# Fixed places for the fourth stage's split down weights, earlier decodings in the second stage, and two seams filled differently

## The chip, the core and the metric

The kernel runs on one core of one Trainium2 chip. A core has a matrix engine (TensorE, called PE in the rows), a vector engine (VectorE, DVE), a scalar engine (ScalarE, ACT), GpSimd (POOL) and a queue engine that issues transfers (SyncE, SP). Each engine works through its own list of instructions in order and waits on semaphores for the others. The metric is the device time of one execution in microseconds; less is better.

## The reference, cut to what matters

Three computations follow one another: a block-wise linear attention with decay, a mixture of four experts with ReLU, and a feed-forward block with SiLU.

```python
x = attention(q, k, v, lam)                 # 1536 tokens x 512
for e in range(4):                          # _moe_ref
    h = np.maximum(x @ w1[e], 0.0)          # 512 -> 1024
    out += p[:, e:e + 1] * (h @ w2[e])      # 1024 -> 512
h = out @ w_in                              # _moe2_ref, 512 -> 2048
g = h * (1.0 / (1.0 + np.exp(-h)))
return g @ w_out                            # 2048 -> 512
```

## The kernel before

All matmuls run in the fp32r format with each float32 operand split in two: a rounded high half and the rest as a low half. A product is then three matmuls (high by high, low by high, high by low). A **split** (`split`, line 145) is two instructions: ScalarE copies the source into the high half (line 149), and GpSimd, or VectorE, subtracts it from the source to give the low half (line 150). Every split therefore takes a place in ScalarE's list and one in GpSimd's.

The 1536 tokens are worked in four stages, which follow one another. Stage "a" does the mixture for the first 512 tokens, stage "c" the mixture for the other 1024, stage "b" the feed-forward for the first 512, stage "d" the feed-forward for the other 1024. In the order of time they are the first (a), second (c), third (b) and fourth (d). Stages c and d use a scheme with seven products instead of eight for a 2 by 2 block product.

Stage c has 16 steps. Its first eight run `pair_step` (line 823), the other eight `pair7` (line 1007), and stage d has eight steps of `pair7`. A step has seven **gaps**, 0 to 6. In each gap TensorE does one product of six matmuls (into a bank called x, z, y, y, z, x, y in turn), the step's own copies and vector work on that bank follow ("then" and "later" in the code), extra jobs given by the caller for that gap run (`prepare`), and then usually one **filler**: `filler` (line 744) takes the next down-projection piece from the list `fill` and lets TensorE do it. The third argument of `pair7` gives the number of fillers per gap. In gap 0 ScalarE copies x to y (line 1052), in gap 1 it copies z to s5 and in gap 2 y to s16 (line 1018); TensorE may go on with y in gap 2 only after the copy of gap 0, and with y in gap 3 only after the copy of gap 2. The four banks are handed on from step to step, so a step's x can begin when the former step's z has been read for the last time. At the end of a step the gated results are split as operands by `operand` (line 936): ScalarE makes the high half (line 940), VectorE or GpSimd the low half (line 942).

`unit` (line 736) is a clock that every product and every filler moves on by one; `after(n, fn)` lists `fn` to be issued n units later. The order of instructions on every engine is therefore written out by hand by the place of each call.

For `pair7` the down weights are first combined by `down_sums` (line 905, four GpSimd operations a step) and then split by `down_left(q)` (line 921; two copies on ScalarE and two subtractions on GpSimd for each q). Two steps make a group with seven such pieces, q = 7g to 7g+6. Each piece goes into one of six buffers used in turn, and the group's products (`down7`, line 966) are the fillers of the next two steps. `seven` (line 883) sets when pieces, sums and loads are issued: it ties them to units after the group's fillers, so that a piece can come ahead of the copy of gap 0 or of a sigmoid.

In the first eight steps of stage c the kernel also decodes weights of the last block from 64 bit words. `decode_next` (line 254) stores the result of the decoding before, loads words ahead and has ScalarE scale the upper words; `flush` (line 230) then issues the four VectorE instructions of the decoding (lines 207, 210, 213, 217). Fourteen decodings fall into stage c. Before the change they start in gap 4 of step 0, gaps 1 and 4 of steps 1 to 6, and gap 1 of step 7, and are flushed in gaps 0 and 3.

Between stages c and b (line 1338 on) the accumulated result is split into xhi and xlo, four columns each, and is then the moving operand of stage b's first product (`gemm1`, line 553). Six fillers stand between, three more follow stage b's first product and three its second; there a fourth call finds the list empty.

Of the kernel before, what the change touches and what calls it, by code (L numbers as in the profile page):

```python
# [31 lines left out]
NV = NF  # L32
# [7 lines left out]
def kernel(  # L40
# [97 lines left out]
    def load(j, n=1):  # L138
        for _ in range(n):
            if nxt[j] < len(seq[j]):  # L140
                ph, i, src = seq[j][nxt[j]]
                nxt[j] += 1
                (load_up, load_down)[j](src, i, (ph, i))
# [110 lines left out]
    def decode_next(more):  # L254

        if jobs[0] < 4 * NV:
            store_decoded()
            if more:
                load_next()
            pending.append(decode(jobs[0]))  # L260
            jobs[0] += 1
# [460 lines left out]
    def left_in2(i):  # L722
        t = leftp.tile([P, 2, 2, HW], F32R, tag="uc", name="uc")
        for n in range(2):
            nc.sync.dma_start(out=t[:, n].bitcast(F32), in_=wu[i][:, n, :2])
        grp_t[("d", i), 1] = t[:, 0], t[:, 1]
# [6 lines left out]
    def after(n, fn):  # L733
        due.append((clock[0] + n, fn))
# [9 lines left out]
    def filler():  # L744
        if fill:
            fill.pop(0)()
        unit()
# [135 lines left out]
    def seven(ph, first, n):  # L883

        now.update(ph=ph, first=first, groups=n // 2, dw=0, pending=None)
        free["o"] = list(range(9 if ph == "c" else 10))
        for box in (d_sums, dw_t, op_t, acc7, jobs7):
            box.clear()
        for g in range(n // 2):
            q = 7 * g  # L890
            todo = [(0, 1, lambda q=q: down_left(q + 6))]
            more = g + 1 < n // 2
            if more or ph == "c":
                todo.append((0, 5, lambda: load(1, 2)))
            if more:
                todo += [
                    (2, 1, lambda i=2 * g + 2: down_sums(i)),
                    (3, 1, lambda i=2 * g + 3: down_sums(i)),
                ]
                for m, when, n_ in ((4, 2, 7), (5, 2, 8), (5, 2, 9), (6, 1, 10), (6, 3, 11), (6, 5, 12)):  # L900
                    todo.append((m, when, lambda q=q + n_: down_left(q)))
            for m, when, fn in todo:
                jobs7.setdefault(q + m, []).append((when, fn))

    def down_sums(i):

        w = raw_t[(now["ph"], now["first"] + i), 1].rearrange("p n (d c) -> p n d c", c=HW)
        t = tmp["d"].tile([P, 3, HW], F32, tag="ds", name="ds", bufs=2)
        for to, a, b, op in (
            (t[:, 0], w[:, 0, 1], w[:, 1, 1], ALU.add),  # L910
            (t[:, 1], t[:, 0], w[:, 0, 0], ALU.subtract),
            (t[:, 2], w[:, 1, 0], t[:, 1], ALU.subtract),
            (w[:, 0, 1], w[:, 0, 0], w[:, 0, 1], ALU.subtract),
        ):
            nc.gpsimd.tensor_tensor(out=to, in0=a, in1=b, op=op)
        d_sums[i] = {
            1: w[:, 0, 0], 2: w[:, 1, 0], 4: w[:, 1, 1],
            5: t[:, 0], 6: t[:, 1], 3: t[:, 2], 7: w[:, 0, 1],
        }

    def down_left(q):

        turn = now["dw"] % 6
        now["dw"] += 1
        if turn < 2:
            t = tmp["op"].tile([P, 2, DM], F32R, tag="dw", name="dw", bufs=2)
        else:
            tag = ("dh", "dl")[turn % 2]
            t = wp.tile([P, 2, DM], F32R, tag=tag, name=tag)
        t = t.rearrange("p s (k c) -> p s k c", c=HW)  # L930
        for s in range(2):
            src = d_sums[q // 7 * 2 + s][ROUND[q % 7]]
            split(nc.gpsimd, t[:, s, 0], t[:, s, 1], src)
        dw_t[q] = t
# [216 lines left out]
    with tc.manual_schedule():  # L1151
# [149 lines left out]
        for i in range(NW):  # L1301
            jc = jobs_for(("c", i), ("c", i + 1) if i + 1 < NW else None)
            if i % 4 == 3:
                for gap, t in ((5, 1), (6, 0)):
                    jc.setdefault(gap, []).append(lambda t=t: load_gate("c", i // 4 + 1, t))
            if i < SW:
                for gap, fn in ((0, flush), (1, 0), (3, flush), (4, 0)):
                    if not fn:
                        if (i, gap) in ((0, 1), (SW - 1, 4)):
                            continue  # L1310
                        fn = lambda: decode_next(True)
                    jc.setdefault(gap, []).append(fn)
                if i == SW - 1:
                    jc[4].append(store_decoded)
                pair_step("c", i, jc)
                continue
            if i == SW:
                flush()
                store_decoded()
                words.close()  # L1320
                tmp["op"] = pool(ops, "opsp")
                fill[:] = fill[4:8] + fill[:4] + fill[8:]
                jc[4].insert(0, second_form)
                jc[5] = jc.get(5, []) + [lambda: down_sums(0)]
                jc[6] = jc.get(6, []) + [lambda: down_sums(1)]
            elif i == SW + 1:
                for gap, qs in ((0, [0]), (1, [1]), (3, [2]), (4, [3]), (6, [4, 5])):
                    jc.setdefault(gap, []).extend(lambda q=q: down_left(q) for q in qs)
            if i == NW - 1:
                jc[4] = [lambda: split_up(("b", 0), False)]  # L1330
            pair7(i - SW, jc, {SW: [1] * 7, SW + 1: [0, 1, 1, 1, 1, 1, 2]}.get(i))
# [7 lines left out]
        for d in range(KD):  # L1339
            split(nc.gpsimd, y_a[0][:, d], y_a[1][:, d], acc_t["a"][:, d])  # L1340
            if d % 2:
                filler()
        filler()

        nb = len(steps["b"])
        sums = ExitStack()
# [3 lines left out]
        for i in range(nb):  # L1350
            flush()
            gemm1("b", i)
            unit()
            if i < 2:
                for _ in range(3 + i):
                    filler()
            elif i < nb - 2:
                gemm2("b", i - 2)
            if i % 2:
                load(0)  # L1360
                left_out(i // 2)
                for n in ([0, 1] if i == 1 else [i // 2 + 1]):
                    if n < NV:
                        left_kept(n)
                if i == nb - 3:
                    grp_t[("d", 0), 0] = hi, lo = up_tiles(wp)
                    split(nc.gpsimd, hi[:, 0], lo[:, 0], lead[0])
                    split(nc.gpsimd, hi[:, 1:], lo[:, 1:], lead[1])
                if i < nb - 1:
                    split_down(("b", (i + 1) // 2))  # L1370
                else:
                    fill += last_down("b", nb)
                    filler()
            else:
                left_sums(("b", i // 2))
                if i == nb - 2:
                    left_in2(0)
                if 2 <= i < nb - 2:
                    split_up(("b", i // 2 + 1), False)
                if i == nb - 6:  # L1380
                    lead = [
                        leftp.tile([P, 2 * DM], F32, tag="uc", name="lead")[:, :HW],
                        tmp["sums"].tile([P, 4, HW], F32, tag="lead", name="lead"),
                    ]
                    nc.sync.dma_start(out=lead[0], in_=wd[0][0][:, A11 * HW:])
                    nc.sync.dma_start(out=lead[1], in_=wu[0][:, 2])
            if i == 1:
                assert not fill
                ops.close()
                tmp["sums"] = pool(sums, "sums2", side="right")  # L1390
            if i == 2:
                mixing = combine(acc_t["c", 0], acc_t["c", 1])
            elif i > 2:
                for job in mixing[i - 3:i - 2]:
                    job()
# [5 lines left out]
        for i in range(NV):  # L1401
            jobs = {}
            if i + 1 < NV:
                jobs[4] = [left_in(i + 1)]
                jobs[6] = [lambda: left_in2(i + 1)]
            if i == 0:
                jobs[0] = [lambda: down_sums(0)]
                jobs[2] = [lambda: down_sums(1)]
                jobs[5] = [lambda: down_left(0)]
            elif i == 1:  # L1410
                jobs[0] = [lambda: down_left(1)]
                jobs[4].insert(0, lambda: down_left(2))
                jobs[5] = [lambda: down_left(3), lambda: down_left(4)]
                jobs[6].append(lambda: down_left(5))
            pair7(i, jobs, {0: [0, 1, 1, 1, 0, 1, 0], 1: [0, 1, 1, 0, 1, 1, 2]}.get(i))
        fill[-1:] = [
            lambda o=o: down7(NV // 2 - 1, 6, 1, slice(o, o + CW))
            for o in range(0, TW, CW)
# [59 lines left out]
```

## Time and profile before

| | |
|---|---|
| median of three runs | 806.03 us (805.63 to 813.93) |
| the profiled execution | 806.18 us, of which 804.4 us from its first to its last instruction |
| mean granted clock of TensorE | 0.996 of full speed |
| TensorE busy | 785.6 us, 4038 matmuls |
| VectorE busy | 559.9 us, 803 instructions |
| GpSimd busy | 506.5 us, 458 instructions |
| ScalarE busy | 365.5 us, 656 instructions |

The profile page gives the busy time of each engine, its course over the span in 40 slices, the transfers, the chain of work that ended last, the costliest groups of instructions and the transfers by line. The trace behind it can be asked for the instructions in order of time, for the waits of an engine, and for the busy time and the granted clock in a stretch. "po<-ohi,dh" names the tile written and the tiles read; "x2" behind a row means that two equal neighbours were merged; square brackets give the idle time of the engine ahead of the row and what ended it. Times are microseconds from the first instruction.

### The profile page before, as it was taken

What the parts mean: (1) busy time and instruction counts of PE and PEld (TensorE: products, weight loads), DVE (VectorE), ACT (ScalarE), POOL (GpSimd) and SP (SyncE); (2) the same over time, 40 slices, a digit from 0 to 9 for tenths busy, and PEclk for the clock granted to TensorE, in tenths of its full rate; (3) what the DMA queues carried; (4) which work ended last, traced back from release to release, by engine and by line L of the source; (5) the groups of instructions that cost most, each with busy time, mean ns of one, the idle gap of its engine ahead of it and who ended that gap; (6) DMA issues with size and microseconds to landing.
All of it is one profiled execution on the core that took longest, in us unless ns stands there. A gap on an engine that the chain in (4) does not pass through costs nothing.

```text
span 804.4 us, 11063 instructions
## 1 busy us (share of the span) xinstructions
PE 785.6 (98%) x4038; PEld 645.7 (80%) x4038; DVE 559.9 (70%) x803; ACT 365.5 (45%) x656; POOL 506.5 (63%) x458
## 2 busy tenths in 40 slices
PE   9999999999999999998999999999999989999997
PEld 8888888788888888886888888878888767878786
DVE  7345587786685888887787878774555464677776
ACT  3323434324545333333444546463445576555551
POOL 3856646254774555555698988795877754565643
PEclk9999999999999999999999999999999999999999
DMA  7868768542344354332002121117676524232202
GB/s 295 311 221 251 233 212 299 197 156 92 102 161 137 112 158 131 130 103 93 15 27 105 42 90 57 49 52 269 222 260 225 181 87 138 77 100 83 81 1 106
DMA packets 39913, 113.89 MB, mean 142 GB/s; under 512 B 4482, under 2 KB 6706, under 8 KB 39858
## 3 DMA queue, kind: packets, MB, share of 16 engines
q1 hardware_dynamic: 39856, 113.18, 41.6%
q8 instruction: 32, 0.52, 0.3%
q14 instruction: 23, 0.19, 0.1%
q10 hardware_dynamic: 2, 0.00, 0.0%
HBM read 89.02 MB, written 24.14 MB: 141 GB/s over the span
## 4 chain that ended last, share of the span: by engine, by line
PE 73%; DVE 17%; ACT 6%; issue 2%; DMA 1%; POOL 1%; SPq 0%; ACTq 0%; POOLq 0%; DVEq 0%
PE ph L553 16%; PE po L609 16%; PE po L983 14%; PE y L755 8%; PE z L755 5%; PE x L755 5%; PE po L803 4%; DVE acc L817 3%; ACT hhi L782 2%; DVE olo L942 1%; DVE hlo L785 1%; PE s L419 1%; PE xps L458 1%; DVE dec L213 1%; DVE dec L207 1%
## 5 line engine op out<-in xcount | busy, mean ns | idle before, releaser
L150 POOL TENSOR_TENSOR ub<-u,ua 128x1024 fp32r<-128x1024 f32 (+2 forms) x41 | 70.2, 1712 | 107.4 <-ACT ua L149 94.7
L150 POOL TENSOR_TENSOR dl<-d,dh 128x1024 fp32r<-128x1024 f32 (+1 forms) x33 | 79.3, 2403 | 24.9 <-ACT dh L149 24.8
L150 POOL TENSOR_TENSOR ub<-us,ua 128x1024 fp32r<-128x1024 f32 x23 | 55.9, 2432 | 34.6 <-ACT ua L149 34.6
L579 ACT ACTIVATE hhi<-ph 128x512 fp32r<-128x512 f32 x40 | 23.9, 599 | 104.3 <-DVE ph L573 85.7
L947 DVE TENSOR_TENSOR acc<-po,acc 128x512 f32<-128x512 f32 (+1 forms) x77 | 51.8, 677 | 18.2 <-PE po L983 18.0
L609 PE MATMUL po<-hhi,dh 128*128 128x512 f32 (+1 forms) x208 | 57.2, 379 | 0.0
L609 PE MATMUL po<-hhi,dl 128*128 128x512 f32 (+1 forms) x208 | 55.9, 373 | 0.0
L609 PE MATMUL po<-hlo,dh 128*128 128x512 f32 (+1 forms) x208 | 55.9, 372 | 0.0
L553 PE MATMUL ph<-xhi,ua 128*128 128x512 f32 (+1 forms) x208 | 53.3, 378 | 0.7 <-DVE xlo L475 0.7
L553 PE MATMUL ph<-xlo,ua 128*128 128x512 f32 (+1 forms) x208 | 52.4, 373 | 0.4 <-POOL xlo L150 0.4
L553 PE MATMUL ph<-xhi,ub 128*128 128x512 f32 (+1 forms) x208 | 52.3, 373 | 0.0
L803 PE MATMUL po<-hhi,dl 128*128 128x512 f32 x128 | 50.0, 391 | 0.0
L803 PE MATMUL po<-hhi,dh 128*128 128x512 f32 x128 | 50.0, 391 | 0.0
L803 PE MATMUL po<-hlo,dh 128*128 128x512 f32 x128 | 49.9, 390 | 0.0
L580 DVE TENSOR_TENSOR hlo<-ph,hhi 128x512 fp32r<-128x512 f32 x40 | 27.7, 692 | 27.4 <-ACT hhi L579 27.4
L817 DVE TENSOR_TENSOR acc<-po,acc 128x512 f32<-128x512 f32 x56 | 36.9, 681 | 13.9 <-PE po L803 13.9
L149 ACT ACTIVATE dh<-d 128x1024 fp32r<-128x1024 f32 (+2 forms) x52 | 40.1, 791 | 8.7 <-PE po L609 3.6
L553 PEld LDWEIGHTS ph<-xlo,ua 128*128 128x128 f32 x208 | 37.4, 188 | 7.7 <-POOL xlo L150 0.9
L553 PEld LDWEIGHTS ph<-xhi,ua 128*128 128x128 f32 x208 | 36.8, 188 | 8.4 <-ACT xhi L474 0.9
L609 PEld LDWEIGHTS po<-hhi,dl 128*128 128x128 f32 x208 | 37.8, 188 | 7.1
L609 PEld LDWEIGHTS po<-hlo,dh 128*128 128x128 f32 x208 | 37.8, 188 | 7.0
L609 PEld LDWEIGHTS po<-hhi,dh 128*128 128x128 f32 x208 | 37.1, 188 | 7.5 <-issue 0.2
(219 smaller groups left out, 2160.0 us busy)
## 6 DMA issues: line engine op xcount, KB each, us to landing
u<-wts SPq DMA_DIRECT2D x32, 512.0 KB, 3.4
d<-wts SPq DMA_DIRECT2D x32, 512.0 KB, 4.5
words<-wts SPq DMA_DIRECT2D x32, 512.0 KB, 4.5
wd<-dec SPq DMA_DIRECT2D x32, 256.0 KB, 2.7
d<-wd SPq DMA_DIRECT2D x16, 512.0 KB, 3.8
qkt<-qk SPq DMA_DIRECT2D x12, 512.0 KB, 4.5
kvt<-kv SPq DMA_DIRECT2D x10, 512.0 KB, 4.6
u<-wd SPq DMA_DIRECT2D x8, 512.0 KB, 4.1
```

Of the source, the lines that this page charges most:

```text
L149: nc.scalar.activation(out=hi, in_=src, func=AF.Copy)
L150: eng.tensor_tensor(out=lo, in0=src, in1=hi.bitcast(F32), op=ALU.subtract)
L553: nc.tensor.matmul(pt[:, :n], lhsT=w, rhs=x[:, k, o:o + n], start=(j == 0), stop=(j == len(ops) - 1),)
L579: nc.scalar.activation(out=hi, in_=pt, func=AF.Copy)
L580: nc.vector.tensor_tensor(out=lo, in0=pt, in1=hi.bitcast(F32), op=ALU.subtract)
L609: nc.tensor.matmul(po_t[d][:, o:o + n], lhsT=w[:, d * P:(d + 1) * P], rhs=h[:, :n], start=(begin and j == 0), stop=(last and j == 2), skip ...
L755: nc.tensor.matmul(to, lhsT=a[:, k * P:(k + 1) * P], rhs=b[:, k], start=(first and j == 0), stop=(j == len(ops) - 1), skip_group_check=not ...
L782: nc.scalar.activation(out=hi, in_=c, func=AF.Copy)
L803: nc.tensor.matmul(po, lhsT=w, rhs=h, start=(j == 0), stop=(j == len(ops) - 1))
L817: nc.vector.tensor_tensor(out=a, in0=po, in1=a, op=ALU.add)
L947: eng.tensor_tensor(out=out, in0=a, in1=b, op=op)
L983: nc.tensor.matmul(po[:, part], lhsT=w, rhs=h[:, part], start=(fresh and j == 0), stop=(j == len(ops) - 1), skip_group_check=not fresh,)
```

## The change

It has three parts. In stage d, `seven` no longer lists anything; the caller gives every `down_left`, `down_sums` and `load` a gap of its own (`lefts` and `plan`), as a job behind that gap's copies. Pieces 0, 1, 2 and 3 of a group come in gaps 1, 2, 2 and 5 of the odd step ahead of the group, pieces 4, 5 and 6 in gaps 1, 1 and 2 of the even step that follows; the last two pieces come behind the last step. The fillers of step 0 move from gap 3 to gap 6. In stage c every decoding starts one place earlier: step 0 has one more, in gap 6, with a flush in its gap 5; step 6 has one more flush, in gap 6; step 7 has none. Between stages c and b one filler moves from behind stage b's second product to ahead of its first.

```diff
--- before.py
+++ after.py
@@ -886,12 +886,11 @@
         free["o"] = list(range(9 if ph == "c" else 10))
         for box in (d_sums, dw_t, op_t, acc7, jobs7):
             box.clear()
-        for g in range(n // 2):
+        for g in range(n // 2 if ph == "c" else 0):
             q = 7 * g
             todo = [(0, 1, lambda q=q: down_left(q + 6))]
             more = g + 1 < n // 2
-            if more or ph == "c":
-                todo.append((0, 5, lambda: load(1, 2)))
+            todo.append((0, 5, lambda: load(1, 2)))
             if more:
                 todo += [
                     (2, 1, lambda i=2 * g + 2: down_sums(i)),
@@ -1306,11 +1305,16 @@
             if i < SW:
                 for gap, fn in ((0, flush), (1, 0), (3, flush), (4, 0)):
                     if not fn:
-                        if (i, gap) in ((0, 1), (SW - 1, 4)):
+                        if (i, gap) == (0, 1) or i == SW - 1:
                             continue
                         fn = lambda: decode_next(True)
                     jc.setdefault(gap, []).append(fn)
-                if i == SW - 1:
+                if i == 0:
+                    jc[5].append(flush)
+                    jc.setdefault(6, []).append(lambda: decode_next(True))
+                elif i == SW - 2:
+                    jc.setdefault(6, []).append(flush)
+                elif i == SW - 1:
                     jc[4].append(store_decoded)
                 pair_step("c", i, jc)
                 continue
@@ -1340,7 +1344,8 @@
             split(nc.gpsimd, y_a[0][:, d], y_a[1][:, d], acc_t["a"][:, d])
             if d % 2:
                 filler()
-        filler()
+        for _ in range(2):
+            filler()
 
         nb = len(steps["b"])
         sums = ExitStack()
@@ -1352,7 +1357,7 @@
             gemm1("b", i)
             unit()
             if i < 2:
-                for _ in range(3 + i):
+                for _ in range(3):
                     filler()
             elif i < nb - 2:
                 gemm2("b", i - 2)
@@ -1403,16 +1408,24 @@
             if i + 1 < NV:
                 jobs[4] = [left_in(i + 1)]
                 jobs[6] = [lambda: left_in2(i + 1)]
+            lefts = {1: (1,), 2: (2,), 5: (3,)} if i == 1 else {1: (0,), 2: (1, 2), 5: (3,)}
+            if i % 2 == 0:
+                lefts = {1: (4, 5), 2: (6,)} if i else {}
+            elif i == NV - 1:
+                lefts[5] = (3, 4)
+            q = 7 * ((i - 1) // 2)
+            plan = [(gap, lambda n=n: down_left(q + n)) for gap, ns in lefts.items() for n in ns]
             if i == 0:
-                jobs[0] = [lambda: down_sums(0)]
-                jobs[2] = [lambda: down_sums(1)]
-                jobs[5] = [lambda: down_left(0)]
-            elif i == 1:
-                jobs[0] = [lambda: down_left(1)]
-                jobs[4].insert(0, lambda: down_left(2))
-                jobs[5] = [lambda: down_left(3), lambda: down_left(4)]
-                jobs[6].append(lambda: down_left(5))
-            pair7(i, jobs, {0: [0, 1, 1, 1, 0, 1, 0], 1: [0, 1, 1, 0, 1, 1, 2]}.get(i))
+                plan += [(0, lambda: down_sums(0)), (2, lambda: down_sums(1)), (5, lambda: down_left(0))]
+            elif i % 2 == 0:
+                plan += [(3, lambda: load(1, 2)), (5, lambda: down_sums(i))]
+            elif i > 1:
+                plan.append((0, lambda: down_sums(i)))
+            for gap, fn in plan:
+                jobs.setdefault(gap, []).append(fn)
+            pair7(i, jobs, {0: [0, 1, 1, 0, 0, 1, 1], 1: [0, 1, 1, 0, 1, 1, 2]}.get(i))
+        down_left(7 * NV // 2 - 2)
+        after(3, lambda: down_left(7 * NV // 2 - 1))
         fill[-1:] = [
             lambda o=o: down7(NV // 2 - 1, 6, 1, slice(o, o + CW))
             for o in range(0, TW, CW)
```

## Rows read from the trace of the kernel before

**Rows 1.** Page, first part: busy time (share of span) and instructions of each engine.

```profile
PE 785.6 (98%) x4038; PEld 645.7 (80%) x4038; DVE 559.9 (70%) x803; ACT 365.5 (45%) x656; POOL 506.5 (63%) x458
```

**Rows 2.** Waits of TensorE: who for whom, us in total, times, longest.

```profile
PE y L755 <- ACT y L1052: 4.6, 4, 3.0
...
PE po L983 <- DVE acc L947: 1.2, 2, 0.7
```

**Rows 3.** Timeline of TensorE, step 7 to 8 of stage c: start, us, instruction.

```profile
374.50 1.06 PE L755 MATMUL x<-hi,ua 128*128 128x512 f32 x2 [3.80 <-DVE hlo L785]
...
378.25 0.40 PE L803 MATMUL po<-hhi,dh 128*128 128x512 f32 x1
```

**Rows 4.** Timeline of VectorE, steps 2 and 7 of stage c.

```profile
251.43 0.42 DVE L207 TENSOR_SCALAR dec<-words 128x512 uint32<-128x512 uint32 x1
...
252.82 0.69 DVE L217 CUSTOM_DVE_ANT_0 dec<-dec,tail 128x1024 uint16<-128x1024 uint16 x1
...
364.57 2.14 DVE L207 TENSOR_SCALAR dec<-words 128x512 uint32<-128x512 uint32 x1
...
368.29 0.69 DVE L842 TENSOR_TENSOR v<-y,s 128x512 f32<-128x512 f32 x1
...
373.76 0.69 DVE L785 TENSOR_TENSOR hlo<-z,hhi 128x512 fp32r<-128x512 f32 x1 [0.74 <-ACT hhi L782]
```

**Rows 5.** Stretches: us, TensorE busy (matmuls), granted clock, transfer share, GB/s.

```profile
662.00:663.00 1.00, 0.20 (x1) 1.00 1.07 303
...
664.00:665.00 1.00, 0.00 (x0) 0.93 0.93 339
665.00:666.00 1.00, 0.81 (x2) 0.50 0.56 197
```

**Rows 6.** Timeline of all engines, steps 0 and 1 of stage c.

```profile
228.44 2.42 POOL L150 TENSOR_TENSOR ub<-us,ua 128x1024 fp32r<-128x1024 f32 x1 [0.21 <-ACT ua L149]
...
230.44 0.69 DVE L788 SCALAR_TENSOR_TENSOR x<-x,gate 128x512 f32<-128x512 f32 x1
...
230.83 2.40 POOL L150 TENSOR_TENSOR dl<-d,dh 128x1024 fp32r<-128x1024 f32 x1
...
233.13 0.60 ACT L782 ACTIVATE hhi<-y 128x512 fp32r<-128x512 f32 x1 [1.36 <-DVE y L788]
...
237.02 0.62 PE L755 MATMUL y<-hi,ua 128*128 128x512 f32 x2
```

**Rows 7.** Timeline of TensorE, stage b's first product.

```profile
539.84 0.50 PE L553 MATMUL ph<-xlo,ua 128*128 128x512 f32 x1 [0.45 <-POOL xlo L150]
```

**Rows 8.** Timeline of ScalarE and TensorE, steps 1 and 2 of stage d.

```profile
659.95 0.72 ACT L149 ACTIVATE dl<-d 128x256 fp32r<-128x256 f32 x2
660.56 0.60 ACT L628 ACTIVATE acc<-po 128x512 f32<-128x512 f32 x1
...
664.05 0.60 ACT L996 ACTIVATE acc<-po 128x512 f32<-128x512 f32 x1 [2.40 <-DMA out<-acc]
...
665.19 1.22 PE L755 MATMUL y<-hi,ua 128*128 128x512 f32 x2 [3.00 <-ACT y L1052]
```

**Rows 9.** Timeline of TensorE and ScalarE, steps 4 and 5 of stage d.

```profile
699.41 0.62 PE L983 MATMUL po<-hhi,dw 128*128 128x512 f32 x2
...
701.07 0.63 PE L755 MATMUL x<-hi,ua 128*128 128x512 f32 x2
...
707.70 1.32 ACT L149 ACTIVATE dw<-d 128x256 fp32r<-128x256 f32 x4
...
709.57 0.73 PE L755 MATMUL y<-hi,ua 128*128 128x512 f32 x2 [0.66 <-ACT s L1018]
...
721.94 0.61 PE L755 MATMUL x<-hi,ua 128*128 128x512 f32 x2
...
728.74 0.61 PE L755 MATMUL y<-hi,ua 128*128 128x512 f32 x2
```

**Rows 10.** Page, sixth part: transfers by line, KB each, us to landing.

```profile
d<-wd SPq DMA_DIRECT2D x16, 512.0 KB, 3.8
```


## What the change should do to the time

> **What bounds the kernel now.** First the page's busy times: TensorE is busy for 98% of the span [rows 1]. No other engine is near that, and the matmuls are the same after the change, so only TensorE's waits can be won or added, and what the clock loses behind them. Next TensorE's waits over the whole span: 4.6 us for the copy of gap 0 (line 1052), 3.0 of it at once, and 1.2 us for VectorE's additions [rows 2]. The timelines then show where the larger ones lie: 3.80 us between step 7 and 8 of stage c [rows 3], 0.45 us in stage b's first product [rows 7], 3.00 us in step 2 of stage d [rows 8], and small ones at each start of a group in stage d [rows 9]. One block of six matmuls is the unit: from x to the second y in step 5 of stage d are five blocks and no wait, 728.74 − 721.94 = 6.80 us, so 1.36 us a block and 0.227 us a matmul [rows 9].
>
> After the two long waits the clock matters too. Nine matmuls from 374.50 to 378.25 took 3.75 us where full speed gives 9 × 0.227 = 2.04 [rows 3]: 1.7 us more. In step 2 of stage d the granted clock is seen to fall to 0.50, 1.2 instead of 2.4 GHz. The last matmul had ended near 662.2 (busy 0.20 of the microsecond from 662), and the clock was still full until some 0.07 us ahead of 665 (0.93): it fell 2.7 us after the work had stopped [rows 5].
>
> **Stage c, step 7: −4.8.** Step 8's x waits for VectorE's low half of z at 373.76, the end of a chain that begins with v at 368.29, 5.47 us earlier [rows 4]. Ahead of v stood a decoding from 364.57, 3.72 us long, whose first instruction alone took 2.14 [rows 4]. Step 7 now has no decoding. v then waits for TensorE itself: the engine went idle at 374.50 − 3.80 = 370.70, and behind the product that v reads stood four blocks, so this ended near 370.70 − 4 × 1.36 = 365.26. v starts 368.29 − 365.2 = 3.1 us earlier, and x too; 0.7 us of wait are left, too short for a fall, so the 1.7 us come back: 3.1 + 1.7 = 4.8. Bounds: 3.1 (the clock falls anyway) and 5.5 (no wait left).
>
> **Stage c, step 0: +2.0.** The decoding taken from step 7 comes back at the other end. Step 0's flush stands ahead of the gating of x, which ran at 230.44 [rows 6], and nothing on VectorE covers it. Undisturbed a decoding takes 252.82 + 0.6 − 251.43 = 2.0 us [rows 4]. But GpSimd has two splits of 2.4 us in a row there, 228.44 and 230.83 [rows 6], and 2.14 us for an instruction that else takes 0.42 shows VectorE standing still behind such a split [rows 4]. I expect the first instruction when the first split ends (230.86), the second split from 231.2 to 233.5, and the other three (1.6 us) behind it: x is gated at 235.0, 4.6 late. Behind it on VectorE stand the low half of x and the gating of y; ScalarE's high half of y (233.13) moves to 237.7, and in ScalarE's list the copy of step 1's gap 0 is behind that: about 238.2 to 238.8. TensorE wants it at 237.02 [rows 6]: 1.8 us of wait and 0.2 to fill the engine again. Nothing wins this back, since TensorE is the bound. Bounds: an undisturbed decoding lets the copy end near 236.2, so 0; GpSimd's second split going first as well gives 2.2. I take 2.0, since the row with such a split beside it (2.14) is nearest.
>
> The Trainium skill speaks against this place (SBUF — State Buffer, "SBUF: two separate sides"): the port pair that VectorE and GpSimd share is a lock which an instruction holds to its end while the other one stands still. The 2.14 us agree; the page does not say who goes next, and if GpSimd did, the sum would be 797.5 instead of 797.3.
>
> Step 6's new flush runs about 355.4, ahead of the gating of y, in 2.0 us. The y copy of step 7 is 3 blocks ahead of its use, which hides it; without that cover it would cost up to 2.0. The other decodings keep their places with another job in them, nothing. In SP's queue one store and one load of words move ahead in step 0; behind them stand only loads for the next step, nothing.
>
> **Between c and b: −0.5.** One more block ahead of stage b's first product gives GpSimd 1.36 us more for xlo, and the wait was 0.45 [rows 7], with its restart 0.5. Behind the second product one block fewer stands; the operands there were split long before. Bounds 0 and −0.7.
>
> **Stage d, steps 0 to 2: −2.2.** The filler moved from gap 3 to gap 6 lets x and z of step 1 start earlier, but the second y then waits for the same copy to s16, ahead of which ScalarE has the same copies and one piece as before: nothing, bounds −0.6 and +0.3. In step 2 the 3.00 us go back to ScalarE, blocked at 664.05 for 2.40 us by the output transfer that frees the accumulator; this transfer starts behind the copy at 660.56 [rows 8]. That copy stood behind one piece (659.95, 0.61 us), which now comes later, and the pieces of gaps 4 and 5 ahead of it delayed it by about another 0.5 (one pair of copies, 0.6, less some slack; an estimate). So transfer, accumulator and y copy come 1.1 us earlier. TensorE's idle time shrinks to about 2.3 us, under the 2.7 after which the clock fell [rows 5]; I take it that the clock stays and about 1.5 us come back (seven matmuls at half speed, 7 × 0.227, the eighth in part). Pieces 4 and 5, four copies of together 1.3 us [rows 9], now stand ahead of s16: 0.4 lost. −1.1 − 1.5 + 0.4 = −2.2; bounds −0.7 (the clock falls) and −2.6.
>
> **Steps 3 to 7 and the end: −3.2.** Step 4 takes 709.57 − 701.07 = 8.50 us for the five blocks that take 6.80 in step 5, and its last filler ahead of x takes 701.07 − 699.41 = 1.66 instead of 1.36 [rows 9]: 2.0 lost, and step 6 has the same plan. The 0.3 and the wait for the copy of gap 0 come from pieces ahead of ScalarE's sigmoid of x and ahead of that copy; both move behind. The wait for s16 (0.66) stays, because four copies (1.32) still stand ahead of it [rows 9]. So 2.0 − 0.8 = 1.2 won in each, 2.4. In steps 5 and 7 one piece is new ahead of s16, 0.15 each: +0.3; in step 3 slack covers it. At the end the same earlier sigmoid wins 0.3 and the first of VectorE's late additions (0.7, restart 0.1 [rows 2]): −1.1. Buffers: a piece reuses the one six pieces before, whose last filler always runs at least one gap earlier, nothing. SP: the loads of down weights stay in gap 3, nothing; if they came late, see below. Together −3.2, bounds 0 and −3.8.
>
> **Sum.** −4.8 + 2.0 − 0.5 − 2.2 − 3.2 = −8.7. The profiled execution took 806.18 us (span 804.4, 1.8 around it): 797.5; the median of the runs is 0.15 lower, so 797.3.
>
> **Rivals.**
> - The decoding in step 0 costs nothing: VectorE is not stopped by the second split. For it, most decodings run beside GpSimd without TensorE waiting; against it, the 2.14 [rows 4]. 797.3 − 2.0 = 795.3. Chance 0.2.
> - The clock falls after the shorter idle times all the same, in stage d (+1.5), and perhaps in stage c (+1.7): 798.8 to 800.5. For it, 2.3 is not far below 2.7; against it, it has been seen only after more. Chance 0.18.
> - The fixed places only exchange waits: what leaves the copy of gap 0 goes to s16 and to the operands' high halves, behind which pieces now queue in gap 5. Steps 3 to 7 win nothing, 797.3 + 3.2 = 800.5. For it, ScalarE has the same copies in sum; against it, step 5, which had few pieces ahead of its copies and no wait. Chance 0.13.
> - Slower: the pieces' copies wait in ScalarE's list for the down weights and their sums, with all copies behind them, in steps 3, 5 and 7. The weights are asked for in gap 3 of the even step and read first in gap 1 of the odd one, ten blocks or 13.6 us later, and take 3.8 [rows 10]; GpSimd's sums lie between. To cost all 8.7, each step has to lose 2.9: it decides from weights and sums ready 12.7 us late instead of 3.8 after the issue plus 13.6 − 3.8 = 9.8 of slack, less the sums. Then 806 and more. Chance 0.04.
>
> **How the numbers follow.** The forecast has 0.45, its own range 796.2 to 798.6. The range goes from the free decoding to both falls or the exchanged waits, 794.8 to 800.5, and leaves out no more than 2 in 10. A measurement of this kernel tells about 1% (8.06 us) from no change; that is 797.97, close above the forecast. Faster by more: about 0.3 of the 0.45 and the 0.2, so 0.5; within 1%: 0.46; slower: 0.04.
>
> **What would show it.** Step 7: no line 207 from 358 on, step 8's x near 371 and a granted clock of 1.00 behind it. Step 0: line 207 at 230.5 standing behind a split, and a wait of TensorE for line 1052 near 237. Stage b: no wait for xlo. Stage d: line 996 still waiting for the transfer, about 1.1 us earlier, the clock at 1.00; no wait for line 1052 in steps 4 and 6, but one of about 0.7 for line 1018. The prediction is wrong if TensorE waits in step 0 or 1 of stage c for longer than 2.6 us, or in steps 3, 5 or 7 of stage d behind a piece.

## The result, and the profile after

The changed kernel took 798.11 us (median of 20 runs, 795.98 to 805.53) against 806.14 us for the kernel before in the same runs (805.43 to 813.93): a ratio of 0.989, 95% interval 0.986 to 0.992. The forecast was 797.3 (range 794.8 to 800.5). The profiled execution has a span of 796.4 us instead of 804.4. In the profiles of five experiments below a VectorE instruction stands for 7 to 8 us, in one of them twice (last section), and by their times some executions of every kernel here seem to hold such a standstill, so stretches are compared, not spans, and a time called undisturbed leaves those executions out.

The page's busy times of after, and the longest of TensorE's waits over its span (who for whom, us in total, times, longest; a line of before between 894 and 1308 has a number smaller by one in after):

```profile
PE 781.7 (98%) x4038; PEld 644.6 (81%) x4038; DVE 557.2 (70%) x803; ACT 365.0 (46%) x656; POOL 502.9 (63%) x458
```

```profile
PE y L755 <- ACT y L1051: 2.8, 2, 2.2
PE y L755 <- ACT s L1017: 1.8, 3, 0.7
PE y L755 <- ACT y L833: 1.6, 1, 1.6
...
PE x L755 <- DVE hlo L785: 0.9, 1, 0.9
...
PE po L982 <- DVE acc L946: 0.5, 1, 0.5
```

Against [rows 1, 2] TensorE's 4038 matmuls fill 781.7 us instead of 785.6. Of these 3.9 us, 1.6 are matmuls behind step 7 that ran at the slow clock before (below). The rest was not traced in full; a matmul's end is modelled, so part of a wait counts as busy (the wait listed as 0.45 in [rows 7] is 0.61 from start to start, as worked out below for the part between c and b). Of the four waits for the copy of gap 0, 4.6 us, two are left, 2.8 us; the 3.80 us between steps 7 and 8 of stage c [rows 3] have become 0.9; one wait of 1.6 us (line 833) is new.

TensorE does the same matmuls in both kernels, so the start of the same matmul in the two traces tells at each point how far after is ahead. The last column is what the part in between gave:

| up to, in TensorE's list | start before | start after | ahead | forecast of the part | measured |
|---|---|---|---|---|---|
| stage c, step 0, last filler ahead of the late y | 236.80 | 236.54 | −0.26 | – | −0.26 |
| first filler behind that y | 238.38 | 239.99 | +1.61 | +2.0 | +1.87 |
| step 8, z | 378.95 | 375.81 | −3.14 | −4.8 | −4.75 |
| stage b, a product at 589 | 589.18 | 585.25 | −3.93 | −0.5 | −0.79 |
| stage d, step 2, last filler ahead of the late y | 661.81 | 657.62 | −4.19 | ↓ | −0.26 |
| step 2, y of gap 3 | 669.47 | 664.60 | −4.87 | −2.2 (with the row above) | −0.68 |
| last accumulation but one | 800.21 | 792.25 | −7.96 | −3.2 | −3.09 |

The sum is −8.0 instead of −8.7, and one part carries the difference: stage d, steps 0 to 2, gave 0.94 instead of 2.2. The 0.26 of the first row lies ahead of everything that the change touches.

**Stage c, step 7.** Timelines of VectorE and TensorE of after:

```profile
366.73 0.70 DVE L842 TENSOR_TENSOR v<-y,s 128x512 f32<-128x512 f32 x1 [0.73 <-PE y L755]
...
372.19 0.69 DVE L785 TENSOR_TENSOR hlo<-z,hhi 128x512 fp32r<-128x512 f32 x1 [0.74 <-ACT hhi L782]
...
372.94 0.72 PE L755 MATMUL x<-hi,ua 128*128 128x512 f32 x2 [0.87 <-DVE hlo L785]
...
375.13 0.39 PE L803 MATMUL po<-hhi,dh 128*128 128x512 f32 x1
```

In step 7 no line 207 stands ahead of v any more; v now waits for TensorE itself (its releaser is "PE y"). The chain from v to z's low half still takes 372.19 − 366.73 = 5.46 us, as in [rows 4]. The wait is 0.87 instead of 3.80, and the nine matmuls behind it take 375.13 − 372.94 = 2.19 us; in before they took 3.75 [rows 3]. The clock stayed, with 1.00 granted in each of the three microseconds from 373. It is so in all ten traces: the three that keep the wait of 3.8 us (before, and below "stage d alone" and "the filler alone") have the fall behind it, the seven with 0.9 have none.

**Stage c, step 0.** GpSimd, VectorE, ScalarE and TensorE of after, in order of time:

```profile
228.18 2.42 POOL L150 TENSOR_TENSOR ub<-us,ua 128x1024 fp32r<-128x1024 f32 x1 [0.20 <-ACT ua L149]
230.19 0.69 DVE L207 TENSOR_SCALAR dec<-words 128x512 uint32<-128x512 uint32 x1
230.57 2.57 POOL L150 TENSOR_TENSOR dl<-d,dh 128x1024 fp32r<-128x1024 f32 x1
230.81 2.62 DVE L210 TENSOR_SCALAR tail<-words 128x512 uint32<-128x512 uint32 x1
233.34 0.68 DVE L213 SCALAR_TENSOR_TENSOR dec<-words,dec 128x512 uint32<-128x512 uint32 x1
...
234.67 0.69 DVE L788 SCALAR_TENSOR_TENSOR x<-x,gate 128x512 f32<-128x512 f32 x1
...
237.35 0.60 ACT L782 ACTIVATE hhi<-y 128x512 fp32r<-128x512 f32 x1 [0.82 <-DVE y L788]
237.85 0.59 ACT L833 ACTIVATE y<-x 128x512 f32<-128x512 f32 x1
...
238.49 0.73 PE L755 MATMUL y<-hi,ua 128*128 128x512 f32 x2 [1.56 <-ACT y L833]
```

The second of the decoding's four instructions stands for 2.62 us and ends 0.3 us after GpSimd's second split does (233.14). Everything behind it moves as the forecast said: x is gated at 234.67, against 230.44 in [rows 6], the y copy of line 833 starts at 237.85 and TensorE waits 1.56 us. The forecast had named line 1052 for this wait; that copy belongs to `pair7`, and `pair_step`, which runs here, has its own at line 833.

**Stage d, step 2.** ScalarE, SyncE and TensorE of after, and the stretches of a microsecond around the late y (us, TensorE busy, granted clock, transfer share, GB/s):

```profile
655.70 0.59 ACT L628 ACTIVATE acc<-po 128x512 f32<-128x512 f32 x1
656.32 0.34 SPq L629 DMA_DIRECT2D out<-acc  x1
...
659.03 0.60 ACT L995 ACTIVATE acc<-po 128x512 f32<-128x512 f32 x1 [1.87 <-DMA out<-acc]
659.53 0.59 ACT L1051 ACTIVATE y<-x 128x512 f32<-128x512 f32 x1
...
660.17 1.22 PE L755 MATMUL y<-hi,ua 128*128 128x512 f32 x2 [2.17 <-ACT y L1051]
```

```profile
658.00:659.00 1.00, 0.00 (x1) 1.00 1.02 215
659.00:660.00 1.00, 0.00 (x0) 1.00 0.88 312
660.00:661.00 1.00, 0.83 (x2) 0.59 0.67 242
661.00:662.00 1.00, 1.00 (x3) 0.50 0.09 32
```

The copy that starts the transfer runs at 655.70 instead of 660.56 [rows 8]; less the 3.8 us that TensorE is ahead at step 1, that is 1.1 us earlier, as forecast. The wait shrinks from 3.00 to 2.17. But the clock falls again, to 0.50, and the 1.5 us that were to come back with it did not.

### The profile page after: what moved, and what is told of

It reads as the page before. It is cut to its first block, busy times and chain, and to the rows that moved or that the text cites. A ratio compares the mean times of both kernels' runs of the same rounds, so it can differ in the third digit from the quotient of the medians.

```text
span 796.4 us, 11068 instructions
## 1 busy us (share of the span) xinstructions
PE 781.7 (98%) x4038; PEld 644.6 (81%) x4038; DVE 557.2 (70%) x803; ACT 365.0 (46%) x656; POOL 502.9 (63%) x458
## 4 chain that ended last, share of the span: by engine, by line
PE 85%; DVE 6%; ACT 4%; issue 2%; DMA 1%; POOL 1%; SPq 0%; ACTq 0%; DVEq 0%
PE po L982 17%; PE ph L553 15%; PE po L609 14%; PE po L803 11%; PE y L755 11%; PE z L755 6%; PE x L755 6%; PE s L419 2%; PE xps L458 1%; DVE olo L941 1%; ACT ohi L939 1%; PE xps L454 1%; DVE s L946 1%; DVE sg L946 1%; PE xps L487 0%
## 5 line engine op out<-in xcount | busy, mean ns | idle before, releaser
L553 PEld LDWEIGHTS ph<-xhi,ub 128*128 128x128 f32 x208 | 37.4, 188 | 7.0
```

The lines of the kernel that those rows point to most:

```text
L553: nc.tensor.matmul(pt[:, :n], lhsT=w, rhs=x[:, k, o:o + n], start=(j == 0), stop=(j == len(ops) - 1),)
```

## The experiments

After was not run beside the kernels below. The kernel before was, and took 807.12 us beside the first four and 806.79 beside the other four, against 806.14 beside after. So a difference of about 1 us between the medians of after and of an experiment shows nothing by itself; there the traces decide.

### Each part alone

**The decodings alone.** The kernel before with only the change in stage c:

```diff
-                        if (i, gap) in ((0, 1), (SW - 1, 4)):
+                        if (i, gap) == (0, 1) or i == SW - 1:
...
+                if i == 0:
+                    jc[5].append(flush)
+                    jc.setdefault(6, []).append(lambda: decode_next(True))
+                elif i == SW - 2:
+                    jc.setdefault(6, []).append(flush)
```

> The kernel before with the earlier decodings of stage c alone. Theory (the parts add up; step 7's wait of 3.8 us and the slow matmuls behind it are won, a wait of 1.6 us in step 1 is paid): 4.8 won, 1.8 lost, so 3.0 us less than the kernel before, near 803.1, and the profile shows TensorE waiting 1.6 us for line 833 near 237 and about 0.9 us for a low half of x at step 8, with the clock at full speed there. Rival (the decodings' gain comes from the stages behind, and stage c alone only moves the wait from step 8 to step 1): within 1 us of the kernel before, near 805.5.

Measured: 802.68 (12 runs, 801.01 to 811.2), before 807.12 beside it; ratio 0.996 (0.9925 to 0.9995). That is 4.4 us less where 3.0 were expected, but the interval, 0.4 to 6.0 us, holds both. TensorE of this kernel, at steps 0 and 8:

```profile
239.41 0.73 PE L755 MATMUL y<-hi,ua 128*128 128x512 f32 x2 [1.57 <-ACT y L833]
...
373.86 0.72 PE L755 MATMUL x<-hi,ua 128*128 128x512 f32 x2 [0.88 <-DVE hlo L785]
```

Both waits are those of after to a hundredth: gain and loss belong to the decodings, and neither needs the rest of the change. In its trace step 0 costs 1.9 us and step 7 gives 4.7, as in after.

**Stage d alone.** After, with the decodings and the filler between c and b as in before:

```diff
-                        if (i, gap) == (0, 1) or i == SW - 1:
+                        if (i, gap) in ((0, 1), (SW - 1, 4)):
...
-        for _ in range(2):
-            filler()
+        filler()
...
-                for _ in range(3):
+                for _ in range(3 + i):
```

> The kernel before with the fixed places of stage d alone. Theory (pieces behind the copies take away the waits for the copy of gap 0 at each group's start and the late sigmoid of x; the wait for the output transfer stays): 4.1 us less, near 802.0, of it 3.1 in steps 3 to 7 and the end, 1.0 in steps 0 to 2; if the clock stays up in step 2, 1.4 us less again. Rival (the waits are only exchanged, line 1052 against line 1018): within 1 us of the kernel before in steps 3 to 7, near 805.

Measured: 801.64 (7 runs, 799.76 to 815.29), ratio 0.993 (0.989 to 0.997). TensorE of this kernel, with step 2's late y, the next y, and the y of gap 3 in step 4; and two stretches behind the first:

```profile
678.23 0.72 PE L755 MATMUL y<-hi,ua 128*128 128x512 f32 x2 [2.02 <-ACT y L1051]
...
681.46 0.73 PE L755 MATMUL y<-hi,ua 128*128 128x512 f32 x2 [0.19 <-ACT s L1017]
...
720.34 0.73 PE L755 MATMUL y<-hi,ua 128*128 128x512 f32 x2 [0.51 <-ACT s L1017]
```

```profile
678.00:679.00 1.00, 0.77 (x3) 1.00 0.83 294
679.00:680.00 1.00, 1.00 (x6) 1.00 0.05 18
```

Steps 4 and 6 behave as in after (no wait for line 1051, one of half a microsecond for line 1017). Step 2 behaves as the forecast said and after's profile did not: the clock stays at 1.00, and behind it a small wait for s16 shows. From the product at 589 of the table above to the y of gap 3 in step 2 this kernel takes 77.75 us, before 80.29 and after 79.35: 2.5 won where the forecast had 2.2.

**The filler alone.** The kernel before with only this:

```diff
-        filler()
+        for _ in range(2):
+            filler()
...
-                for _ in range(3 + i):
+                for _ in range(3):
```

> The kernel before with the filler between stages c and b alone. Theory: TensorE's wait for xlo (0.45 us listed, 0.7 from start to start) goes and nothing else: 0.7 us less, near 805.4. Rival (stage b's third product, with one filler fewer ahead of it, waits for the split of its own weights instead): no change, 806.1.

Measured: 810.84 (12 runs, 805.01 to 818.28), ratio 1.001 (0.998 to 1.005). By time this is inconclusive: the interval is wider than the 0.7 us in question. The trace decides: it has no wait of stage b's product for GpSimd's low half any more, and none in its place, and the stretch from the last fillers of stage c (527.67 in before) to the product at 589 takes 60.75 us instead of 61.51, exactly as in after: 0.76 won.

### What costs 1.8 us in step 0

Two edits move one of the two things that met there: the decoding, or the second of GpSimd's two splits.

**The extra decoding in step 5** (after, changed so):

```diff
-                if i == 0:
-                    jc[5].append(flush)
-                    jc.setdefault(6, []).append(lambda: decode_next(True))
+                if i == SW - 3:
+                    jc.setdefault(6, []).extend([flush, lambda: decode_next(True)])
```

> The changed kernel, with the extra decoding in gap 6 of step 5 instead of step 0 (both its flush and its start), where GpSimd has no split. Theory (step 0's cost comes from VectorE's decoding standing behind two splits of GpSimd ahead of the gating of x): the 1.6 us wait for line 833 goes and none takes its place, 1.8 us less than the changed kernel, near 796.3. Rival (any third decoding ahead of a gating makes the next step's copy late by its 2 us, wherever it stands): a wait of 1 to 2 us appears at step 6's gap 2 instead and the time stays near 798.1.

Measured: 796.38 (6 runs, 794.57 to 803.24), ratio 0.987 (0.983 to 0.992). No wait for line 833 is left, and no new one of its size took its place. In its trace 1.86 us are won in step 0, and 0.35 are lost again at the first y of step 7 (360.19), where the copy of line 833 now comes just too late.

**The splits of step 0 earlier** (after, changed so; `split_down` is the second of the two splits, with its copy on ScalarE, and the first stays):

```diff
-            jobs[5 if key[1] < SW - 1 else 3] = [lambda: split_down(key)]
+            jobs[5 if 0 < key[1] < SW - 1 else 3] = [lambda: split_down(key)]
...
-                    jc[5].append(flush)
+                    jc.setdefault(5, []).append(flush)
```

> The kernel after, with the GpSimd splits of step 0 of the second stage in gap 3 instead of 5, so that the second of them does not stand beside VectorE's early decoding; the decoding and the flush stay in gap 5. Theory (GpSimd's splits on the same operands' memory hold VectorE's decoding up, each by its own length): the decoding takes about 2.3 us less, the wait for y at step 1 falls to 0.3 or less, 1.6 to 1.8 us less than after: near 796.4. Rival (the decoding's own 2 us ahead of the gating is what costs): a wait of more than 1 us stays, 798.1.

Measured: 798.73 (4 runs, of which the two undisturbed took 795.34 and 796.71), ratio 0.988 (0.983 to 0.993). By time this is too few runs; the trace decides. GpSimd, VectorE and TensorE of this kernel at the same place:

```profile
228.20 2.41 POOL L150 TENSOR_TENSOR ub<-us,ua 128x1024 fp32r<-128x1024 f32 x1 [0.21 <-ACT ua L149]
230.21 0.69 DVE L207 TENSOR_SCALAR dec<-words 128x512 uint32<-128x512 uint32 x1
230.82 0.41 DVE L210 TENSOR_SCALAR tail<-words 128x512 uint32<-128x512 uint32 x1
...
232.48 0.69 DVE L788 SCALAR_TENSOR_TENSOR x<-x,gate 128x512 f32<-128x512 f32 x1
...
236.79 0.62 PE L755 MATMUL y<-hi,ua 128*128 128x512 f32 x2
```

The decoding starts at the same time, in the same place of VectorE's list, and delays the gating of x by 2.3 us instead of 4.5: its second instruction takes 0.41 instead of 2.62, and TensorE waits for nothing. Not the decoding's own 2 us are the price, but the split of GpSimd that runs beside it. Not every VectorE instruction pays it: in before the gating of x (230.44) ran beside the same two splits in its usual 0.69 us [rows 6].

### What is left in stage d

**An accumulator of its own** (after, changed so; the place that stage d's first accumulator shares with stage b's output is what the transfer has to free):

```diff
-                acc_t["d"] = accp.tile([P, KD, TW], F32, tag="acc", name="acc")
+                acc_t["d"] = tmp["d"].tile([P, KD, TW], F32, tag="accd", name="acc")
```

> The kernel after, with the fourth stage's accumulator in a tile of its own instead of the place that the output still being transferred holds. Theory (the wait of TensorE for y at step 2, 2.2 us in after, goes back to the output transfer through the accumulation on VectorE, and the slow clock behind it costs the rest of the 4.0 us of slips there): the accumulation no longer waits for the transfer, the wait and the slow stretch go, a wait of 0.4 to 0.9 for the copy of s appears at steps 1 and 2, so about 3.3 us less than after: near 794.8. Rival (the copies of y are late by ScalarE's own work, or by the PSUM place, and the transfer is only the last of several): another wait of like size takes its place, and the time stays at 798.

Measured: 795.68 (8 runs, 794.57 to 803.35), ratio 0.984 (0.980 to 0.987). The transfer was named right as cause, with one word of the expectation wrong: the accumulation that waited is ScalarE's line 995, not VectorE's. ScalarE and TensorE of this kernel:

```profile
664.65 0.59 ACT L995 ACTIVATE acc<-po 128x512 f32<-128x512 f32 x1
665.13 0.61 ACT L1051 ACTIVATE y<-x 128x512 f32<-128x512 f32 x1
...
665.79 0.73 PE L755 MATMUL y<-hi,ua 128*128 128x512 f32 x2 [0.21 <-ACT y L1051]
...
669.48 0.73 PE L755 MATMUL y<-hi,ua 128*128 128x512 f32 x2 [0.67 <-ACT s L1017]
```

Line 995 waits for nothing, and TensorE 0.21 us instead of 2.17. Behind it the wait for s16 shows in full, 0.67. The gain is smaller than expected, though: the median is 2.4 under after's instead of 3.3. In the traces the 13 matmuls from the last filler ahead of that y to the y of gap 3 take 4.29 us instead of 6.98, 2.7 less, and where after's clock stays up there is less to win (table below).

**Piece 5 in gap 2** (after, changed so):

```diff
-                lefts = {1: (4, 5), 2: (6,)} if i else {}
+                lefts = {1: (4,), 2: (5, 6)} if i else {}
```

> The kernel after, with piece 5 of an even step's splits in gap 2, behind piece 6's place, so that one piece and not two stands in gap 1. Theory (the waits of 0.5 to 0.7 us for the copy of s at the even steps of the fourth stage come from the piece that stands ahead of it on VectorE): they shrink at steps 4 and 6, about 1.0 to 1.2 us less than after: near 797.0. Rival (the copy of s is late by its own chain from the hidden product, whatever stands ahead): no change, 798.1.

Measured: 797.10 (6 runs, 794.25 to 802.49), ratio 0.987 (0.983 to 0.991): 1.0 us under after's median, which by itself could be chance. The trace decides: the y of gap 3 in step 4, which waited 0.50 us at 703.35 in after, starts without a wait at 708.15 here, and so does that of step 6 (746.74). The waits came from the pieces ahead of the copy; the rival fell. The place is ScalarE's list, which the expectation called VectorE's: in after four copies of line 149 stand there from 701.49 to 702.72, here two.

**All three** (the extra decoding in step 5, the accumulator, piece 5):

> The kernel after with the extra decoding and the flush moved to step 5 of the second stage (as in the earlier run that did this alone), the fourth stage's accumulator in a tile of its own, and piece 5 of the even steps in gap 2. Theory (three separate stalls at three places): the gains add, 1.8 + 3.3 + 1.2 less than after, 791.5 to 792. Rival (they share a cause, or one stall takes another's place): 793.5 or more.

Measured: 791.80 (6 runs, 791.02 to 797.2), ratio 0.980 (0.976 to 0.984): faster than both kernels. The waits of TensorE in it:

```profile
PE x L755 <- DVE hlo L785: 0.9, 1, 0.9
PE y L755 <- ACT y L1051: 0.8, 2, 0.6
PE po L982 <- ACT hhi L939: 0.8, 1, 0.8
PE z L755 <- DVE sg L946: 0.7, 1, 0.7
PE y L755 <- ACT s L1017: 0.7, 1, 0.7
```

The longest wait in the stages c, b and d is 0.9 us. The median lies 6.3 us under after's, with 6.3 expected. Step by step in the traces: 1.5 us are won in stage c as by the extra decoding alone, 3.6 in stage d up to the y of gap 3 in step 2 (the accumulator alone: 2.9), and 1.0 behind it (piece 5 alone: 1.1). So the gains add, and 0.6 come on top: piece 5 in gap 2 also takes away most of the wait for s16 that the accumulator had laid bare (0.07 instead of 0.67). That the sum met the expectation to a tenth is luck, since the accumulator had been put too high.

## Why the prediction was right, and where it was not

**TensorE as the only bound: right.** Every gain and loss found is a wait of TensorE or its clock behind one.

**Step 7, −4.8: right (−4.75)**, by both of its terms: v released by TensorE, and the slow matmuls gone.

**Step 0, +2.0: right (+1.87)**, and so is the mechanism, which was the least certain, in its order too. The first instruction of the decoding, 0.42 us when undisturbed [rows 4], takes 0.69 and ends at 230.88, 0.28 us after the first split (230.60); the second split follows, and the second instruction ends at 233.43, 0.29 after it (233.14). The 2.14 us on which the forecast rested [rows 4] ended at 366.71, likewise 0.28 after this split of before:

```profile
364.03 2.40 POOL L150 TENSOR_TENSOR dl<-d,dh 128x1024 fp32r<-128x1024 f32 x1 [0.57 <-ACT dh L149]
```

x is gated at 234.67; less the 0.26 that after is ahead there, it is 4.5 late, forecast 4.6. The Trainium skill (SBUF — State Buffer, "SBUF: two separate sides") says that the shared port pair is held for a whole instruction while the other engine stands still; the 2.62 us beside a split, and the 0.41 us without it, agree. The sum had gone by VectorE getting one instruction in between the two splits, and the sum of 797.5 by none: it got one.

**Between c and b, −0.5: right in kind, measured −0.79.** The wait and its restart are gone, but the wait was read too small. The three matmuls ahead of it in before:

```profile
538.55 0.84 PE L553 MATMUL ph<-xlo,ua 128*128 128x512 f32 x3
```

The last of them starts at 539.00 and the next matmul at 539.84 [rows 7], 0.84 us later instead of 0.23: from start to start the wait is 0.61. The 0.45 are counted from the modelled end of a matmul, 0.39 us long. With the restart, 0.1 (the matmul behind it starts at 540.18, 0.34 later), this accounts for 0.7 of the 0.76 that the filler alone gives.

**Steps 0 to 2 of stage d, −2.2: wrong in size (−0.94).** The step that failed is "I take it that the clock stays", drawn from one fall seen 2.7 us after the work had stopped [rows 5]. The term for the transfer held: it came 1.1 us earlier, of which 0.26 are spent by TensorE's being there earlier and 0.83 shorten the wait. (Less 1.1, the idle time of 3.0 should have been 1.9; the 2.3 of the forecast does not follow from its own terms. It was 2.17.) The term for the clock, −1.5, came out as +0.15: from the late y to the y of gap 3, 12 matmuls that take 2.72 us at full speed took 4.28 in before (665.19 to 669.47) and 4.43 in after (660.17 to 664.60). One fall gives no limit, as the same place in the other traces shows. Measured from the last filler ahead of the late y to the y of gap 3, 13 matmuls that take 2.95 us at full speed:

| kernel | wait of the late y | clock fell | the 13 matmuls |
|---|---|---|---|
| before | 3.00 | 2.7 us after the last matmul | 7.66 |
| filler alone | 2.83 | no | 6.09 |
| decodings alone | 2.89 | 4.4 us after it, TensorE at work again | 7.29 |
| after | 2.17 | 2.2 us after it | 6.98 |
| extra decoding in step 5 | 2.25 | 2.7 us after it, TensorE at work again | 7.08 |
| splits earlier | 2.33 | no | 5.94 |
| piece 5 in gap 2 | 2.23 | no | 5.51 |
| stage d alone | 2.02 | no | 5.64 |
| own accumulator | 0.21 | no | 4.29 |

With waits of 2.0 to 3.0 us the clock fell in some executions and in others not, and 2.83 without a fall beside 2.17 with one shows that the length alone does not decide. Where it stayed, the stretch took 5.5 to 5.9 us, and the forecast's 7.66 − 2.2 = 5.46 is near that; where it fell, the change won 0.7 at most. Steps 0 to 2 as a whole, from the product at 589 on, gave 2.5 (stage d alone) and 2.2 (splits earlier) in the two kernels that have after's stage d unchanged and kept the clock, as the 2.2 of the forecast. The forecast's 0.4 for s16 is paid only where the clock stays, and was nearer 0.2 (the 0.19 in stage d alone): behind a slow y its copy is early enough. After's own runs fit this: of its 14 undisturbed ones, seven took 795.98 to 797.19 with a mean clock of 1.000, seven 797.89 to 798.25 with 0.997 or 0.998. The medians, 796.87 and 798.14, lie 1.3 us apart, as do 7.08 and 5.94 in the table (1.1). That the lower seven are those without a fall is inferred from the mean clock, since only one execution of after was profiled. So the rival "the clock falls all the same", put at 0.18, is about half of the executions; it moves the time by 1.3 us, and the forecast, 797.3, stands between the two. That the measured median came within 1 us of it is in part luck: a forecast with the clock always kept, or always lost, would have missed one half of the executions. All undisturbed executions together have medians of 806.04 before and 797.54 after, 8.5 apart.

**Steps 3 to 7 and the end, −3.2: right (−3.09).** The waits for the copy of gap 0 in steps 4 and 6 are gone, those for s16 stay at 0.50 and 0.56, and one of VectorE's two late additions is gone. The rival in which fixed places only exchange waits would have left this at nothing, and the slower one, pieces that queue for late weights, left no wait in steps 3, 5 or 7.

Between the forecast's −8.7 and the trace's −8.0 thus lies the 1.3 that stage d's first steps fell short, less two small surpluses, 0.3 ahead of the change and 0.3 between c and b (the other parts differ by 0.1 at most).

What stays open: why the clock falls in one execution and not in the next at a wait of the same length. No edit here could hold the wait and change only that.

## What to carry to other kernels

Before work is put on VectorE at a place where nothing waits yet, look at what GpSimd does at that moment: here a decoding of 2 us held the next instruction up by 4.5 beside a split and by 2.3 after the split was moved, and moving either was enough. A wait that ends with a transfer which frees a buffer is better taken away by a buffer of its own than shortened; shortening it from 3.0 to 2.2 us left the clock to chance, and removing it won 2.7 us more in the traces (6.98 to 4.29). Where an idle time is only shortened, here to 2.0 to 2.9 us, count its gain without the clock, and the clock as a coin to be tossed.

## What had not been expected of the hardware

A VectorE instruction with both inputs in SBUF, which else takes 0.7 to 1.1 us, can be held up through a whole series of GpSimd instructions. GpSimd, VectorE and TensorE of the kernel with its own accumulator, in step 8 of stage c, which is the same code as in after:

```profile
411.28 1.31 POOL L941 TENSOR_TENSOR hlo<-sg,hhi 128x512 fp32r<-128x512 f32 x1
411.99 7.28 DVE L941 TENSOR_TENSOR hlo<-s,hhi 128x512 fp32r<-128x512 f32 x1
412.54 1.45 POOL L150 TENSOR_TENSOR dh<-d,dh 128x256 fp32r<-128x256 f32 x2
...
417.97 0.75 POOL L690 TENSOR_TENSOR us<-u 128x256 f32<-128x256 f32 x1
418.80 1.05 POOL L690 TENSOR_TENSOR us<-us,u 128x256 f32<-128x256 f32 x1
...
422.75 1.22 PE L755 MATMUL y<-hi,ua 128*128 128x512 f32 x2 [4.24 <-ACT s L1017]
```

and the same place in after's profiled execution:

```profile
411.58 1.12 DVE L941 TENSOR_TENSOR hlo<-s,hhi 128x512 fp32r<-128x512 f32 x1
412.10 1.90 POOL L150 TENSOR_TENSOR dh<-d,dh 128x256 fp32r<-128x256 f32 x2
```

In after the engines alternate: VectorE gets its turn, and the GpSimd pair beside it takes 1.90 instead of 1.45. In the execution with the accumulator VectorE stands until 419.27 while GpSimd's instructions follow each other without a gap, up to the first pause of 0.08 us (417.97 + 0.75 = 418.72 to 418.80). TensorE then waits 4.24 us, its clock falls, and the execution is 7 to 8 us longer than undisturbed ones. The same instruction stood for 7.23 us in the filler alone and in stage d alone and for 7.28 with piece 5 in gap 2, and one like it for 7.81 in the decodings alone and in stage d alone, each time up to the same pause. Not one of the five other profiles holds such a standstill. What decides between alternating and standing was not tried; a kernel that gives GpSimd pauses in such a series would tell.
